# The last group's outputs in a buffer of their own, queries turned in pairs, one batch's loads held for another transfer, and a new order, in a fused linear-attention and gated-FFN kernel

## The chip, the cores and the metric

One core of one Trainium2 chip runs the whole program. The time is device microseconds of one execution. The kernel before took 301.0 us, the median of three runs (300.68 to 301.04).

## What is computed

Eight batches of eight heads, 576 positions, 64 values per head. Linear attention with cosine and sine weights, then a gated feed-forward layer over all 4608 tokens (512 wide, 1536 hidden):

```python
r = np.maximum(x, 0.0); phi = np.concatenate([r * c, r * s], axis=-1)   # for q and k
kv  = np.einsum('bhsf,bhsd->bhfd', k_p, v)
z   = np.sum(k_p, axis=2)
num = np.einsum('bhsf,bhfd->bhsd', q_p, kv)
den = np.einsum('bhsf,bhf->bhs', q_p, z)[..., None] + 1e-06
x   = (num / den).transpose(0, 2, 1, 3).reshape(B * S, H * D)
g   = x @ w_gate
out = (g * (1.0 / (1.0 + np.exp(-g))) * (x @ w_val)) @ w_out
```

Inputs and outputs are float32; the products run in 16-bit types with float32 sums.

## The kernel before, in words

**Tiles and groups.** Attention makes 36 token tiles of 128 tokens (two slots of 64; a batch has nine slots, so tile t holds slots 2t and 2t+1). Four tiles are a group of 512 tokens, and the feed-forward layer runs by group, 0 to 8. The gate, value and output products of the later groups are block products with seven instead of eight quarter products (a Strassen form): VectorE makes sums of the weights, of `xT` (L949) and of the hidden tiles (L1092), and TensorE accumulates into PSUM banks that ScalarE first fills with copies (L627).

**The path of a batch b from 2 on.** GpSimd issues the loads of k, v (L120) and q (L125), casting to bf16 on the way. ScalarE applies ReLU to k (L280), VectorE weighs v with the cosine/sine table (`vmul`, L292, four instructions a batch), TensorE makes the key-value products (`kv_job`, L715), ScalarE copies these into SBUF (L627, four copies). The features of q go into a buffer `r_q` (L866, L876, L282), and one DMA transpose from SyncE turns them into `phit` (L838). Then TensorE makes a tile (L784), ScalarE its denominator (L796), VectorE the reciprocal (L802) and the quotient `x` (L806, one of four slots), and SyncE's DMA transpose makes `xT` (L746). The products of a group read `xT` (L976 for block products, L1051 for whole ones).

**Tiles 4 to 8** belong to batches 0 and 1. Their queries are not turned by DMA: `turned_tile` has TensorE transpose 8 pieces of 128x64 for one tile into one bank (L1296), then ReLU (L280 or L282) and a weighting (L1310). In the program before, the turns of tiles 4 and 5 already stand next to each other; those of 6 and 7 stand apart.

**Held loads.** GpSimd's queue is in order. `hold_job` puts a 1x2 copy (L823) on it that reads something a transfer writes, so the loads behind it are issued only when that transfer has landed. The loads of batch 3 (k, v) and of batch 4 (q) are held for `phit` of batch 2.

**Outputs.** A group ends with seven output products (`out_jobs`, L1141). For the last group, products 6, 5 and 3 are split into two halves (P6, P5, P3 below), and VectorE and ScalarE bring the quarters into `ob` (L1184, L1198, L633, L629). `ob` has two places, each for a pair of tiles, used by every group in turn; a place is free when the stores of its last user have landed. Groups 1 to 7 store from GpSimd (L1110), the last group from SyncE and ScalarE (`store_two_jobs`, L1236). The quarter called `e11` in `out_jobs` comes from ScalarE, the two halves `e12` of the last product from VectorE.

**The order.** From the middle of group 0 on, the order of every engine's instructions is made when the program is built. Each piece of work is a `Job` with a duration for each engine that may run it, the jobs it follows, and the rooms (banks, slots, `ob` places) it takes and gives back. TensorE's jobs have keys that give a nominal order; due times are worked back from them, and a list scheduler (`order_once`) places all jobs, with a model of the DMA queue and with due times shifted at random by seeds. Only the order is kept: on the chip each engine runs its instructions in that order and waits on semaphores where data or room is missing.

Of the kernel before, what the change touches and what calls it, by code (L numbers as in the profile page):

```python
# [19 lines left out]
def kernel(  # L20
# [585 lines left out]
    def pe(occ, fn, key, **kw):  # L606
        return Job({"PE": occ}, fn, key=key, **kw)
# [135 lines left out]
    def turn_job(t, x, after, by_pe=False, key=None):  # L743
        if not by_pe:
            def fn(j):
                nc.sync.dma_start_transpose(out=xT_of(t), in_=one(x_all, x))  # L746
            J_["xT", t] = Job({"SP": 1450}, fn, after=after + J_.get(("xT_read", t // OUT - 3), []), put=[x], tail=X_LAND, dma=(1900.0, X_SVC))
            return
        r = Room("bank")

        def fn(j):
            ps = bank(r).bitcast(FP16).rearrange("p (k x) -> p k x", x=P)
            for kc in range(KC):
                nc.tensor.transpose(out=ps[:, kc], in_=one(x_all, x)[:, kc * P:(kc + 1) * P], identity=ident16)
# [61 lines left out]
    def load_job(b, nm, after, lands, behind):  # L816
        def fn(j):
            (load_turned if nm == "q" else load)(b, nm)
        J_["load", b, nm] = Job({"POOL": 1600 if nm == "q" else 780}, fn, after=after, tail=lands, behind=behind, dma=(2500.0, 3500.0))

    def hold_job(read, after):
        def fn(j):
            nc.gpsimd.tensor_copy(out=hold2, in_=read())  # L823
        jb = Job({"POOL": 480}, fn, after=after)
        jb.hold = True
        return jb

    def batch_jobs(b, key):
        def loaded(nm):
            return [J_["load", b, nm]] if b > 2 else []  # L830

        def landed_at(nm):
            return 0.0 if b > 2 else LOADED[nm, 2]
        phis = feature_jobs(b)

        def fn(j):
# [3 lines left out]
        turned = [Job({"SP": 7500}, fn, after=phis + J_.get(("tiles", b - 2), []), tail=PHI_LAND - 7500, dma=(2800.0, 6400.0))]  # L840
# [263 lines left out]
    def store_jobs(t, after, put, queues, cols=slice(0, d_model)):  # L1104
        for e in range(2):
            q_ = queues[e]

            def fn(j, e=e):
                idx = 2 * t + e
                {"POOL": nc.gpsimd, "SP": nc.sync, "ACT": nc.scalar}[j.eng].dma_start(  # L1110
                    out=out_v[idx // NC, idx % NC][:, cols], in_=ob_of(t)[e * SH:(e + 1) * SH, cols])
            Job({q_: 560}, fn, after=after, put=put, tail=6500.0, dma=(1900.0, 500.0))

    obs = {}

    def ob_of(t):
        return ob_all[:, obs[t // 2].at[0], t % 2]
# [113 lines left out]
    def store_two_jobs(t, cols, after, queues):  # L1231
        for e in range(2):
            def fn(j, e=e):
                (b, c), (b1, _) = divmod(2 * t + e, NC), divmod(2 * t + 2 + e, NC)
                assert b == b1
                {"SP": nc.sync, "ACT": nc.scalar}[j.eng].dma_start(  # L1236
                    out=out_v[b, c:c + 3:2, :, cols].rearrange("c p f -> p c f"),
                    in_=pair_of(t // 2)[e * SH:(e + 1) * SH, :, cols])
            Job({queues[e]: 560}, fn, after=after, tail=3000.0)

    def plain_out_jobs(key):
        rooms = [Room("ob"), Room("ob")]
# [39 lines left out]
    kv_job(1, (0, KV1_AT / 16), rk + vm)  # L1282
    plain_out_jobs((0, 0.76, 0.015))

    def turned_tile(t, key):

        r = Room("bank")
        slots = [(0, NC - 1), (1, 0)] if t == 4 else [(1, 2 * t - 9), (1, 2 * t - 8)]
        mine = late[:, 2 * (t % 2):2 * (t % 2) + 2]

        def fn(j):
            ps = bank(r).bitcast(BF16).rearrange("p (y e s) -> p y e s", e=2, s=SH)
            for jj in range(J):
                for n, (b, c) in enumerate(slots):
                    for i in range(2):
                        nc.tensor.transpose(out=ps[i * D:(i + 1) * D, 2 * jj + n].rearrange("p e s -> p (e s)"),  # L1296
                                            in_=raws[b, "q"][:, 2 * jj + i, c], identity=ident)
        mm = pe(240, fn, key, after=[], get=[r], rel=LOADED["sa" if t < 6 else "sb", 1])
        for b, c in slots:
            J_.setdefault(("q_read", b), []).append(mm)  # L1300
        old = J_["tile_mm"][-2:-1] if t > 5 else []

        def fn(j):
            relu_on(j.eng, mine[:, 0].rearrange("p e j c s -> p e (j c) s"),
                    bank(r).bitcast(BF16).rearrange("p (y e s) -> p e y s", e=2, s=SH)[:, :, 0:2 * J])
        re_ = Job({"ACT": sc(512), "DVE": 352}, fn, after=[mm] + old, put=[r])
        c0 = NC - 1 if t == 4 else 2 * t - 9

        def fn(j):
            tt(out=mine[:, 1].rearrange("p e j c s -> p (e j) (c s)"), in0=mine[:, 0].rearrange("p e j c s -> p (e j) (c s)"),  # L1310
               in1=tanT[:, c0:c0 + 2].rearrange("p c s -> p (c s)").unsqueeze(1).to_broadcast([P, 2 * J, P]), op=ALU.mult)
        J_["turned tile", t] = [re_, Job({"DVE": d2(512)}, fn, after=[re_])]

    J_["tile_mm"] = []
    for t in range(4, 9):
        turned_tile(t, (0, (HALF_AT[t - 4] - 0.6) / 16) if t < 8 else (0, T8_AT / 16))
        tile_jobs(t, (0, HALF_AT[t - 4] / 16) if t < 8 else (1, 1.0), t < 8)
        J_["tile_mm"].append(J_["tiles", 1][-1])
    J_["kvd_free"] = J_["tile_mm"][0:1]

    def fn_t(n):
# [53 lines left out]
    def batch_loads(read, after, names):  # L1375
        prev = [hold_job(read, after)]
# [58 lines left out]
    TILES_AT_ONCE = 2  # L1435
    DMA_MARGIN = 0.0
    EARLY = 9000.0
    SIZE = {"sg": NSG, "m7": NM7, "x": NX, "ob": 2, "tile": TILES_AT_ONCE}
    AHEAD = 18000.0
    SLACK = 1600.0  # L1440
    LOOSE = 8000.0
# [11 lines left out]
    def order_once(nominal, seeds):  # L1453
# [89 lines left out]
        while n_left:  # L1543
# [72 lines left out]
    SEEDS = (9809, 17028, 79282, 23851, 85677, 79440, 78841, 69575, 80126, 93490, 42418, 59393, 0, 20917, 95217, 13415, 85644, 62013, 51029, 24021, 0, 84984, 14392, 87705, 77482, 88068, 0, 0)  # L1616
    SHAKE = 1500.0
    WINDOW = 10000.0
    PACK = True
# [40 lines left out]
```

## Time and profile before

| what | value |
|---|---|
| time, median of three runs | 301.0 us (300.68 to 301.04) |
| the profiled execution's own time | 300.46 us |
| span in its profile | 298.7 us |
| granted TensorE clock | 0.998 |
| TensorE (PE) busy | 291.3 us, 98% |
| VectorE (DVE) busy | 250.9 us, 84% |
| ScalarE (ACT) busy | 199.5 us, 67% |
| GpSimd (POOL) busy | 70.6 us, 24% |
| first real product of TensorE / end of the last | 9.0 us / 293.4 us |
| key-value products of batch 3, start | 85.0 us |

The span runs from the first to the last instruction; 1.8 us of the execution's own time lie outside it. Matmuls are pipelined, so the distance from one start to the next tells more than a busy share: four products of 256 columns take 0.437 us from start to start when nothing holds them, four of 512 columns 0.863 us. Idle time in brackets stands before an instruction, with what ended it.

### The profile page before, as it was taken

What the parts mean: (1) busy time and instruction counts of PE and PEld (TensorE: products, weight loads), DVE (VectorE), ACT (ScalarE), POOL (GpSimd) and SP (SyncE); (2) the same over time, 40 slices, a digit from 0 to 9 for tenths busy, and PEclk for the clock granted to TensorE, in tenths of its full rate; (3) what the DMA queues carried; (4) which work ended last, traced back from release to release, by engine and by line L of the source; (5) the groups of instructions that cost most, each with busy time, mean ns of one, the idle gap of its engine ahead of it and who ended that gap; (6) DMA issues with size and microseconds to landing.
All of it is one profiled execution on the core that took longest, in us unless ns stands there. A gap on an engine that the chain in (4) does not pass through costs nothing.

```text
span 298.7 us, 8071 instructions
## 1 busy us (share of the span) xinstructions
PE 291.3 (98%) x3244; PEld 238.4 (80%) x3244; DVE 250.9 (84%) x513; ACT 199.5 (67%) x421; POOL 70.6 (24%) x126
## 2 busy tenths in 40 slices
PE   8999999999999999999999999999999999999992
PEld 4697465676777888888988888888888898888882
DVE  7878996978977898989979997988879868976972
ACT  6664346979558986797699588996475556645520
POOL 7954620030042130221233203200220050002020
PEclk9999999999999999999999999999999999999999
DMA  7999999999989999269899892770370074002025
GB/s 259 228 196 198 202 206 208 201 217 204 193 137 172 157 213 160 72 126 189 131 177 234 143 155 69 145 160 2 73 142 2 0 131 83 2 2 70 2 70 142
DMA packets 71781, 40.89 MB, mean 137 GB/s; under 512 B 48704, under 2 KB 68672, under 8 KB 71744
## 3 DMA queue, kind: packets, MB, share of 16 engines
q0 software_dynamic: 24992, 24.91, 49.8%
q1 hardware_dynamic: 46320, 15.08, 27.1%
q8 instruction: 25, 0.41, 0.6%
q10 hardware_dynamic: 432, 0.39, 0.4%
q14 instruction: 12, 0.10, 0.1%
HBM read 37.75 MB, written 9.44 MB: 158 GB/s over the span
## 4 chain that ended last, share of the span: by engine, by line
PE 88%; DVE 5%; DMA 4%; ACT 1%; issue 1%; ACTq 0%; DVEq 0%
PE banks L976 43%; PE banks L1141 23%; PE banks L1250 4%; PE banks L437 4%; PE banks L903 4%; DMA xT<-x 3%; PE banks L715 2%; PE banks L784 2%; PE banks L1051 2%; DMA wo_sb<-in_v_dram 1%; DVE ht L1060 1%; DVE sums L1092 1%; DVE v L292 1%; PE banks L778 1%; PE banks L371 1%; ACT sg L1035 1%
## 5 line engine op out<-in xcount | busy, mean ns | idle before, releaser
L1110 POOL DMA_DIRECT2D out_dram<-ob x56 | 29.4, 533 | 148.6 <-ACT ob L629 104.7
L1035 ACT ACTIVATE sg<-banks 128x512 bf16<-128x512 f32 x72 | 41.3, 596 | 9.9 <-PE banks L976 9.5
L627 ACT COPY banks<-banks 128x512 f32<-128x512 f32 (+1 forms) x53 | 30.2, 577 | 17.8 <-PE banks L1141 6.0
L1071 DVE TENSOR_TENSOR ht<-sg,banks 128x512 f16<-128x512 bf16 x60 | 40.3, 680 | 1.7 <-PE banks L976 1.6
L976 PEld LDWEIGHTS <-wg_sb 128*128 128x128 f16 x384 | 36.9, 98 | 5.5 <-issue 0.4
L1141 PEld LDWEIGHTS <-ht 128*128 128x128 f16 x384 | 37.0, 98 | 4.9 <-issue 0.3
L976 PEld LDWEIGHTS <-wgs_sb 128*128 128x128 f16 x368 | 35.6, 98 | 5.5
L996 DVE TENSOR_TENSOR banks<-m,banks 128x512 f32<-128x512 f32 x44 | 30.3, 691 | 7.0 <-ACT m L627 4.3
L629 ACT ACTIVATE ob<-banks 128x512 f32<-128x512 f32 x34 | 19.9, 595 | 22.7 <-PE banks L1141 22.3
L976 PEld LDWEIGHTS <-wv_sb 128*128 128x128 f16 x320 | 31.2, 98 | 3.9 <-DVE x L806 0.2
L976 PE MATMUL banks<-kvt,wgs_sb 128*128 128x256 f16 x236 | 33.6, 273 | 0.0
L1141 PEld LDWEIGHTS <-sums 128*128 128x128 f16 x288 | 27.9, 98 | 3.6 <-DVE sums L1092 0.2
L627 ACT COPY m<-banks 128x512 f32<-128x512 f32 x44 | 25.6, 589 | 6.5 <-PE banks L976 6.4
L976 PE MATMUL banks<-xT,wg_sb 128*128 128x256 f16 x192 | 28.5, 273 | 0.3 <-ACT banks L627 0.3
L1141 PE MATMUL banks<-wo_sb,ht 128*128 128x256 f16 x192 | 25.9, 273 | 0.0
L1141 PE MATMUL banks<-wt_sb,sums 128*128 128x256 f16 x192 | 24.3, 273 | 0.0
L976 PE MATMUL banks<-xT,wv_sb 128*128 128x256 f16 x160 | 23.9, 273 | 0.0
L806 DVE TENSOR_TENSOR x<-banks,rec 128x512 f16<-128x512 f32 x32 | 21.7, 687 | 2.0 <-DMA xT<-x 0.3
L976 PE MATMUL banks<-kvt,wg_sb 128*128 128x256 f16 x168 | 23.1, 273 | 0.0
L1141 PE MATMUL banks<-wt_sb,ht 128*128 128x256 f16 x192 | 22.8, 273 | 0.2 <-DVE banks L1184 0.2
L876 ACT ACTIVATE r_q<-raw_q,tanq 128x256 bf16<-128x256 bf16 x45 | 20.1, 503 | 0.0
L1035 ACT ACTIVATE sg<-m 128x512 bf16<-128x512 f32 x24 | 15.1, 629 | 7.1 <-DVE m L1004 7.0
(157 smaller groups left out, 542.4 us busy)
## 6 DMA issues: line engine op xcount, KB each, us to landing
out_dram<-ob POOLq DMA_DIRECT2D x56, 128.0 KB, 3.4
raw_kv<-in_k_dram POOLq DMA_DIRECT2D x7, 576.0 KB, 6.9
raw_q<-in_q_dram POOLq DMA_DIRECT2D x12, 288.0 KB, 9.6
raw_kv<-in_v_dram POOLq DMA_DIRECT2D x6, 576.0 KB, 8.9
out_dram<-ob SPq DMA_DIRECT2D x13, 128.0 KB, 2.5
wg_sb<-in_moe_w_gate_dram POOLq DMA_DIRECT2D x5, 256.0 KB, 8.8
wv_sb<-in_moe_w_val_dram POOLq DMA_DIRECT2D x5, 256.0 KB, 9.4
wo_sb<-in_v_dram SPq DMA_DIRECT2D x2, 576.0 KB, 4.1
```

What stands on the lines that cost most here:

```text
L437: nc.tensor.matmul(out=st["f", tg, fc, lo][i], lhsT=(wg_sb, wv_sb)[i][:, kc, fs], rhs=xT[tg][:, ts, kc], start=(kc == 0), stop=(kc == KC - 1))
L627: nc.scalar.copy(out=out, in_=in_)
L629: nc.scalar.mul(out=out, in_=in_, mul=mul)
L806: tt(out=one(x_all, x).rearrange("p (y e d) -> p e y d", e=2, d=D), in0=view()[:, :, :, 0:D], in1=rec_all[:, t % 4].rearrange("p (e y) o - ...
L876: nc.scalar.activation(out=home()[:, :, c, 1], in_=raws[b, "q"][:, :, c], func=AF.Relu, scale=tanq[:, c:c + 1])
L903: nc.tensor.matmul(out=bank(r), lhsT=w[:, kc, fc * P:(fc + 1) * P], rhs=xT[tg][:, :, kc], start=(kc == 0), stop=(kc == KC - 1))
L976: nc.tensor.matmul(out=to[:, i], lhsT=a[:, c, 2 * u + i], rhs=x()[:, :, c], start=first and i == 0 and c == 0, stop=c == KH - 1, skip_grou ...
L996: tt(out=bank(c), in0=one(m7_all, m).rearrange("p i x -> p (i x)"), in1=bank(b), op=ALU.add)
L1035: nc.scalar.activation(out=gates(rooms[w])[:, :, jh * HT:(jh + 1) * HT], in_=src, func=AF.Silu, scale=DOWN)
L1071: tt(out=ht[:, 4 * u + w:4 * u + w + 3:2, jh * HT:(jh + 1) * HT], in0=gates(rooms[w])[:, :, jh * HT:(jh + 1) * HT], in1=src.rearrange("p ( ...
L1110: {"POOL": nc.gpsimd, "SP": nc.sync, "ACT": nc.scalar}[j.eng].dma_start(out=out_v[idx // NC, idx % NC][:, cols], in_=ob_of(t)[e * SH:(e + ...
L1141: nc.tensor.matmul(out=to, lhsT=a[:, kc, i * P:(i + 1) * P], rhs=b[:, kc], start=first and kc == 0 and i == 0, stop=kc == HC - 1, skip_gro ...
```

## The change

- `rel`, the pool of `r_q`, is gone; `r_q` is a fixed buffer. The last group's outputs go into its first 8192 bytes per partition (`ob_last`, two places of the kind "last ob") and no longer into `ob`.
- `turned_tiles` turns the queries of tiles 4 and 5 in one job into one bank, and those of 6 and 7; tile 8 stays alone.
- The loads of batch 3 (k, v) and of batch 4 (q) are held for `xT` of tile 8, and no longer for `phit` of batch 2.
- The planner's figures for DMA change (durations, landing times, the delay `LATER`), its result counts the ends of all jobs, and the seeds are others. So the order of all engines from 27 us on is another.

TensorE has the same 3245 products and weight loads in both programs. In the new order the key-value products of batch 2 come about 2.5 us earlier, those of batch 3 about 4 us later, of batches 5 and 6 about 12.5 us earlier, of batch 7 about 7 us earlier. On SyncE's queue the turn of batch 5 stands between the transposes of tiles 16 and 19, 18, 17 (before: behind all four), and the transpose of tile 8 stands behind all six of group 0's stores that follow the turn of batch 2 (before: behind five). On GpSimd's queue the hold and the loads of k and v of batch 4 stand ahead of the stores of tiles 4 to 7 (before: between those of 6, 7 and of 4, 5), and k and v of batch 6 ahead of q of batch 6.

```diff
-    rel = ctx.enter_context(tc.tile_pool(name="rel", bufs=1))
+    rq_all = consts.tile([P, G * NC * 2 * D], BF16, name="r_q")
+    ob_last = rq_all[:, 0:8 * d_model].bitcast(FP32).rearrange("p (a b f) -> p a b f", a=2, b=2)
...
-            J_["xT", t] = Job({"SP": 1450}, fn, ..., tail=X_LAND, dma=(1900.0, X_SVC))
+            J_["xT", t] = Job({"SP": 1450}, fn, ..., tail=X_LAND, dma=(1430.0, X_SVC))
...
-    X_LAND = 7000.0
-    X_SVC = 1000.0
+    X_LAND = 4000.0
+    X_SVC = 1030.0
...
-        J_["load", b, nm] = Job(..., dma=(2500.0, 3500.0))
-    def hold_job(read, after):
+        J_["load", b, nm] = Job(..., dma=(1940.0, 2460.0) if nm == "q" else (470.0, 3770.0))
+    def hold_job(read, after, put=()):
...
-        turned = [Job({"SP": 7500}, fn, ..., tail=PHI_LAND - 7500, dma=(2800.0, 6400.0))]
+        turned = [Job({"SP": 7500}, fn, ..., tail=PHI_LAND - 7500, dma=(7600.0, 1370.0))]
...
-                st[b, "q"] = rel.tile([P, G, NC, 2, D], BF16, name="r_q")
+                st[b, "q"] = rq_all.rearrange("p (g c w d) -> p g c w d", g=G, c=NC, w=2)
...
     def pair_of(p):
-        return ob_all[:, obs[p].at[0]]
+        return (ob_last if obs[p].kind == "last ob" else ob_all)[:, obs[p].at[0]]
...
-        rooms = {0: Room("ob"), 1: Room("ob")}
+        rooms = {n: Room("last ob" if last else "ob") for n in range(2)}
...
-    def turned_tile(t, key):
+    def turned_tiles(ts, key):
         r = Room("bank")
...
+        def turned(m):
+            return bank(r).bitcast(BF16).rearrange("p (m y e s) -> p m y e s", m=2, e=2, s=SH)[:, m]
         def fn(j):
+            for m, t in enumerate(ts):
+                for jj in range(J):
+                    for n, (b, c) in enumerate(slots[t]):
+                        for i in range(2):
+                            nc.tensor.transpose(out=turned(m)[i * D:(i + 1) * D, 2 * jj + n].rearrange("p e s -> p (e s)"),
+                                                in_=raws[b, "q"][:, 2 * jj + i, c], identity=ident)
-        mm = pe(240, fn, key, after=[], get=[r], rel=LOADED["sa" if t < 6 else "sb", 1])
+        mm = pe(200 + 236 * len(ts), fn, key, after=[], get=[r], rel=LOADED["sa" if ts[-1] < 6 else "sb", 1])
...
-    for t in range(4, 9):
-        turned_tile(t, ...)
+    for ts in ((4, 5), (6, 7), (8,)):
+        turned_tiles(ts, ...)
...
-            batch_loads(phit_read, J_["turned", b - 1], names)
+            if b == 3:
+                batch_loads(lambda: xT[2][0:1, 0, 0, 0:2], [J_["xT", 8]], names)
+            else:
+                batch_loads(phit_read, J_["turned", b - 1], names)
...
-                j.done = moved[0] + LATER
+                j.done = moved[0] + (j.tail if j.tail < LATER else LATER)
-        return max(j.done for j in jobs if "PE" in j.engs)
+        return max(j.done for j in jobs)
-    LATER = 2200.0
-    SEEDS = (9809, 17028, 79282, 23851, ...)
+    LATER = 2400.0
+    SEEDS = (51094, 66641, 10020, 27923, ...)
```

More of the change, by code (lines that the diff above doesn't have):

```diff
@@ L746, in fn @@
                 nc.sync.dma_start_transpose(out=xT_of(t), in_=one(x_all, x))
-            J_["xT", t] = Job({"SP": 1450}, fn, after=after + J_.get(("xT_read", t // OUT - 3), []), put=[x], tail=X_LAND, dma=(1900.0, X_SVC))
+            J_["xT", t] = Job({"SP": 1450}, fn, after=after + J_.get(("xT_read", t // OUT - 3), []), put=[x], tail=X_LAND, dma=(1430.0, X_SVC))
             return
@@ L818, in fn @@
             (load_turned if nm == "q" else load)(b, nm)
-        J_["load", b, nm] = Job({"POOL": 1600 if nm == "q" else 780}, fn, after=after, tail=lands, behind=behind, dma=(2500.0, 3500.0))
-    def hold_job(read, after):
+        J_["load", b, nm] = Job({"POOL": 1600 if nm == "q" else 780}, fn, after=after, tail=lands, behind=behind, dma=(1940.0, 2460.0) if nm == "q" else (470.0, 3770.0))
+    def hold_job(read, after, put=()):
         def fn(j):
             nc.gpsimd.tensor_copy(out=hold2, in_=read())
-        jb = Job({"POOL": 480}, fn, after=after)
+        jb = Job({"POOL": 480}, fn, after=after, put=put)
         jb.hold = True
@@ L839, in fn @@
                                         in_=st[b, "q"].rearrange("p g c w d -> p (g c w d)"))
-        turned = [Job({"SP": 7500}, fn, after=phis + J_.get(("tiles", b - 2), []), tail=PHI_LAND - 7500, dma=(2800.0, 6400.0))]
+        turned = [Job({"SP": 7500}, fn, after=phis + J_.get(("tiles", b - 2), []), tail=PHI_LAND - 7500, dma=(7600.0, 1370.0))]
         J_["turned", b] = turned
@@ L1238, in fn @@
                     in_=pair_of(t // 2)[e * SH:(e + 1) * SH, :, cols])
-            Job({queues[e]: 560}, fn, after=after, tail=3000.0)
+            Job({queues[e]: 660}, fn, after=after, tail=1300.0, dma=(700.0, 560.0))
     def plain_out_jobs(key):
@@ L1283 @@
     plain_out_jobs((0, 0.76, 0.015))
-    def turned_tile(t, key):
+    def turned_tiles(ts, key):
         r = Room("bank")
-        slots = [(0, NC - 1), (1, 0)] if t == 4 else [(1, 2 * t - 9), (1, 2 * t - 8)]
-        mine = late[:, 2 * (t % 2):2 * (t % 2) + 2]
+        slots = {t: [(0, NC - 1), (1, 0)] if t == 4 else [(1, 2 * t - 9), (1, 2 * t - 8)] for t in ts}
+        def turned(m):
+            return bank(r).bitcast(BF16).rearrange("p (m y e s) -> p m y e s", m=2, e=2, s=SH)[:, m]
         def fn(j):
[L1292 to L1297, printed above, removed]
-        mm = pe(240, fn, key, after=[], get=[r], rel=LOADED["sa" if t < 6 else "sb", 1])
[L1299 to L1312, printed above, removed]
@@ new lines, in turned_tiles, with fn @@
+        mm = pe(200 + 236 * len(ts), fn, key, after=[], get=[r], rel=LOADED["sa" if ts[-1] < 6 else "sb", 1])
+        for t in ts:
+            for b, c in slots[t]:
+                J_.setdefault(("q_read", b), []).append(mm)
+        for m, t in enumerate(ts):
+            mine = late[:, 2 * (t % 2):2 * (t % 2) + 2]
+            old = J_["tile_mm"][t - 6:t - 5] if t > 5 else []
+            def fn(j, m=m, mine=mine):
+                relu_on(j.eng, mine[:, 0].rearrange("p e j c s -> p e (j c) s"), turned(m).rearrange("p y e s -> p e y s"))
+            re_ = Job({"ACT": sc(512), "DVE": 352}, fn, after=[mm] + old, put=[r])
+            c0 = NC - 1 if t == 4 else 2 * t - 9
+            def fn(j, mine=mine, c0=c0):
+                tt(out=mine[:, 1].rearrange("p e j c s -> p (e j) (c s)"), in0=mine[:, 0].rearrange("p e j c s -> p (e j) (c s)"),
+                   in1=tanT[:, c0:c0 + 2].rearrange("p c s -> p (c s)").unsqueeze(1).to_broadcast([P, 2 * J, P]), op=ALU.mult)
+            J_["turned tile", t] = [re_, Job({"DVE": d2(512)}, fn, after=[re_])]
@@ L1319 @@
+    J_["tile_mm"] = []
+    for ts in ((4, 5), (6, 7), (8,)):
+        turned_tiles(ts, (0, (HALF_AT[ts[0] - 4] - 0.6) / 16) if ts[0] < 8 else (0, T8_AT / 16))
+        for t in ts:
+            tile_jobs(t, (0, HALF_AT[t - 4] / 16) if t < 8 else (1, 1.0), t < 8)
+            J_["tile_mm"].append(J_["tiles", 1][-1])
     J_["kvd_free"] = J_["tile_mm"][0:1]
@@ L1373, in gate_order, with batch_loads @@
         return [at["g1"], at["g7"], at["g6"], at["g2"], at["g5"], at["g4"], nxt["g3p"]]
-    def batch_loads(read, after, names):
-        prev = [hold_job(read, after)]
+    def batch_loads(read, after, names, put=()):
+        prev = [hold_job(read, after, put)]
         for b, nm in names:
@@ L1437 @@
     EARLY = 9000.0
-    SIZE = {"sg": NSG, "m7": NM7, "x": NX, "ob": 2, "tile": TILES_AT_ONCE}
+    SIZE = {"sg": NSG, "m7": NM7, "x": NX, "ob": 2, "last ob": 2, "tile": TILES_AT_ONCE}
     AHEAD = 18000.0
```

9 lines of the change are left out of this document (3 added, 6 removed).

## The prediction

> **What bounds the kernel now.** I read the page's busy times and slices first, then TensorE's timeline, then the chain of waits and the timeline of the last 6 us. From the page, busy time (share of the span) and tenths in 40 slices:
>
> ```profile
> PE 291.3 (98%) x3244; PEld 238.4 (80%) x3244; DVE 250.9 (84%) x513; ACT 199.5 (67%) x421; POOL 70.6 (24%) x126
> ...
> PE   8999999999999999999999999999999999999992
> DVE  7878996978977898989979997988879868976972
> ```
>
> TensorE is the bound from the second slice to the last but one. Two things can move the time: TensorE's waits inside the stream, and the ends of the span. As a busy matmul row may hide a wait, I measured waits as the distance from one start to the next beyond the usual distance of the same work. From 26.9 us (the first instruction whose place the change may move) to 293.4 us, five waits exceed 0.16 us: 0.24 at 72.7, 0.34 at 81.7, 0.43 at 86.7, 0.20 at 127.9 and 0.19 us at 128.8, together 1.40 us. From 130 us on there is none beyond 0.1 us before the last products. The first three, in timelines of all engines and of PE (start, length, engine, line; in brackets the idle time and what ended it):
>
> ```profile
> 73.03 0.69 DVE L806 TENSOR_TENSOR x<-banks,rec 128x512 f16<-128x512 f32 x1 [0.26 <-DMA xT<-x]
> 73.77 0.11 PEld L1051 LDWEIGHTS <-wv_sb 128*128 128x128 f16 x2 [0.57 <-DVE x L806]
> ...
> 82.27 2.78 PE L1141 MATMUL banks<-wt_sb,ht 128*128 128x256 f16 x24 [0.17 <-DVE banks L1184]
> ...
> 87.52 0.60 PE L976 MATMUL banks<-xT,wg_sb 128*128 128x256 f16 x4 [0.27 <-ACT banks L627]
> ```
>
> The first is the transfer of tile 8: the chain of waits gives `xT<-x` 8.60 us from 64.31, while the transposes of `xT` land after 2.4/4.5/8.6 us (least, median, most). A quotient needed its slot, a bank came free late, TensorE waited, and VectorE, without a pause until 87 us, was late again at 82.
>
> The end (timeline, same columns):
>
> ```profile
> 293.40 0.42 DVE L633 TENSOR_SCALAR ob<-banks 128x256 f32<-128x256 f32 x1 [0.23 <-PE banks L1141]
> 293.74 0.60 ACT L629 ACTIVATE ob<-banks 128x512 f32<-128x512 f32 x1 [5.41 <-PE banks L1141]
> 293.86 1.28 SPq L1236 DMA_DIRECT2D out_dram<-ob  x2
> 293.90 1.66 ACTq L1236 DMA_DIRECT2D out_dram<-ob  x2
> ```
>
> Read it from the bottom: two queues issue two stores each, and the later store of each carries `e11` (the ScalarE row), which was placed behind the store of the quarter before it because its `ob` place had been the last to come free. The last product ends at 293.37 and its eviction at 293.83; the last store is issued at 294.93.
>
> **Part by part.** The sum is made against the profiled execution (span 298.7, own time 300.46 us), which lies 0.5 us under the median of the runs; differences are carried to that median.
>
> *Own buffer for the last group.* In the changed order ScalarE makes `e11` before it issues any store, and both its stores stand ahead of those of the third and last quarters. The last stores are then the two of `e12`, one on each queue, issued right behind VectorE's 0.42 us, as 293.86 and 293.90 are now. The last issue moves from 294.93 to 293.90: **-1.03 us**. Landing is the same (2.4/2.8/3.0 us for these stores). Ends: nothing, if the two stores' landing were late for another reason; -1.3, if they land at the 2.4 of a quiet queue and not at 2.8.
> The second half of product 2 moves ahead of product 6, so the first half of P5 stands directly behind P6. VectorE needs 0.27 us after P6's first half and 0.43 us (L1184: 288.45 to 288.88), the other half of P6 covers 0.65: **+0.1 us**. The cover is gone if VectorE is behind; it has 0.7 us to spare there, as its last hidden-tile sums follow fewer instructions.
>
> *Turning in pairs.* PE's timeline:
>
> ```profile
> 37.58 0.64 PE L1296 MATMUL banks<-ident,raw_q 128*64 128x128 bf16 x16
> ...
> 43.53 0.39 PE L754 MATMUL banks<-ident,x 128*128 128x128 f16 x4
> 43.85 0.41 PE L1296 MATMUL banks<-ident,raw_q 128*64 128x128 bf16 x8
> 44.20 0.40 PE L754 MATMUL banks<-ident,x 128*128 128x128 f16 x4
> 44.43 0.81 PE L1250 MATMUL banks<-wo_sb,ht 128*128 128x512 f16 x3
> ```
>
> Sixteen pieces in a row (tiles 4 and 5, already neighbours) take 0.56 us to the next start, eight alone 0.35; and the four L754 before a turn take 0.32 instead of the 0.23 of the next four. One pair newly joined: 2 x 0.35 - 0.56 + 0.09 = **-0.2 us**. Its bank is held longer and ReLU reads it twice, as before: two instructions each of ReLU and weighting in both programs, with 0.3 to 0.5 us to spare before tiles 6 and 7.
>
> *Loads of batch 3 held for tile 8.* The first two waits of before (0.58 us) should go. What is late next: the loads themselves. The turn of batch 2 ends its issue at 61.0, six stores of 0.62 follow, tile 8's transpose is issued at 64.9 and lands after the median 4.5 at 69.4; hold 0.18 and 0.36 until the first issue: k at 69.9 (before: 63.85), v at 70.7, q at 71.4 and 72.1. With before's own landing times (7.5, 10.2, 12.0 us) k is there at 77.4, v at 80.9, q at 84.1. GpSimd waits meanwhile; behind it stand only these loads. Before, v had landed 7.3 us ahead of its first use (82.12). Now the cover is thin: on VectorE one weighing of v (0.69) and two sums of `xT` (0.33 each) stand before group 2's second gate product, which PE's stream reaches at 84.1 if nothing waits. v may land at 82.6 at most, 1.7 us later than reckoned. Tiles 10 and 11 are issued at 69.8 and 71.1; even with 8.6 us they land by 79.7. Batch 3's key-value products come 4 us later, which costs nothing by itself.
>
> *Other moves on queues.* Batch 4's hold and loads ahead of four stores (0.53 each): their `ob` place is written again 20 us later. Batch 5's turn ahead of the transposes of tiles 19, 18, 17: it holds SyncE 4.5 to 7.6 us (L838), from about 125.5; tile 17 is issued at 132.6 to 135.7 and lands by 140.2 (4.5), at worst 142.1 (6.4, as after the first loads); its product stands at 141.6: 0 to 0.5 us, taken as 0. Key-value products of batches 5 and 6 move 12.5 us up; k and v of batch 5 landed at 120.4 before, 15 us ahead of the new place. `r_q` as a fixed buffer and the hold's other operand add no instruction.
>
> *The new order.* It places again all work from 27 us on, and what it waits for cannot be seen. Ends: no wait at all (-1.40; PE runs so from 130 to 292 us now), and three stretches like 72 to 87 us, which lost 1.0 us (3.0 us of waits, +1.6). I take the 1.40 us of before, its nearest row: the two waits that go are set against the thin cover of batch 3. **0.**
>
> Sum: -1.03 + 0.1 - 0.2 + 0 = -1.15 us: 299.3 for the profiled execution, and from the median **299.8 us**.
>
> **A rule that speaks against the hold.** Beside tile 8's 8.60 us, the next three transposes took 6.4, 6.1 and 5.4 us with the same loads still in flight. The Trainium skill, "DMA: Bandwidth & Descriptors", section Queues, rings and completion order, says that each DMA engine takes turns between the queues that have work for it, a packet at a time. By it the collision is only moved, to tiles 10 and 11, batch 3's own turn and the loads themselves; the trace agrees as far as it goes. That is the second rival.
>
> **The rivals.**
> *New waits eat it.* For it: ScalarE's and VectorE's work stands close ahead of its users everywhere (batch 3's copies 0.7 us ahead of tile 14, batch 5's 0.2 us ahead of tile 22). Against it: the same was true before, with 1.40 us lost. With 2.2 to 3.2 us of waits: 300.6 to 301.6.
> *Slower: batch 3's values arrive late.* They now share the DMA engines with tiles 10 and 11 and with the turn of batch 3 (issued at 72.4; 9.0 us median). For it: q of batch 3, beside a turn and behind other loads, took 18.1 us. Against: that load had three others ahead, this one has one. Each microsecond beyond 82.6 us is one of TensorE's. It ends slower than before by 0.6 once v lands beyond 84.4 (13.7 us after its issue, instead of 10.2); with 14.5 us the time is 302.4.
> *No waits left.* The new order runs as its stream adds up: 298.4. For it: 160 us of before do. Against: half of that part has no loads any more.
> *The end doesn't shorten.* Another store lands last: 300.9. Against: the four issue times above.
>
> **How the numbers follow.** Three runs of before spread over 0.36 us; 0.2% is 0.6 us, about what a measurement can tell from no change. Forecast (299.0 to 300.4) 0.48, no waits left 0.14: faster 0.62. New waits 0.18 and no shorter end 0.04: same 0.22. Late values: slower 0.16. The range 298.4 to 301.8 takes in the new order's ends and leaves out the outer part of the last rival.
>
> **What would show it.** Tail: ScalarE's last eviction ends before its first store, and last product to last issue falls from 1.6 to 0.5 us. Pairs: L1299's rows in three places (16, 16, 8). Hold: tile 8's transpose lands within 5 us, no VectorE wait on `xT` near 70, loads of batch 3 near 70. Wrong if VectorE waits for `raw_kv` before 84 us or ScalarE for q near 87, with TensorE idle behind, or if TensorE's waits beyond 0.16 us add up to over 2 us.

## The result, and the profile after

The changed kernel took 299.14 us (median of 10 executions, 298.34 to 301.42), the kernel before 301.05 us beside it (10 executions, 300.68 to 301.18): a ratio of 0.9946 with a 95% interval of 0.9923 to 0.9969. It is faster, by 0.3 to 0.8%. The forecast was 299.8 us, a ratio of 0.9960. The profiled execution took 299.61 us with a span of 297.8 us (before: 300.46 and 298.7).

The page of the changed kernel, with the rows of busy time and TensorE's tenths in 40 slices:

```profile
PE 291.9 (98%) x3244; PEld 239.1 (80%) x3244; DVE 252.7 (85%) x513; ACT 199.4 (67%) x421; POOL 71.5 (24%) x126
...
PE   8999999999999999999999999999999999999993
```

TensorE bounds the kernel as before, so the change is to be sought in TensorE's waits and at the ends of the span. I cut the spans (a second profile of the changed kernel comes from its repetition below) at the first instruction that the planner places and at the end of the last product:

| us | before | after | after, second profile |
|---|---|---|---|
| start to the first planned product | 26.91 | 27.75 | 27.41 |
| TensorE's stream from there to the last product's end | 266.46 | 265.47 | 265.24 |
| last product's end to the end of the span | 5.31 | 4.57 | 4.57 |
| span | 298.7 | 297.8 | 297.2 |

The first row is not the change's work: the instructions before 26.9 us are the same in both programs, and the row moves between executions of one kernel (last section). Without it the changed kernel's profiles are 1.7 and 2.0 us shorter, near the 1.9 us between the medians and more than the spans show.

**The end.** Timeline of the changed kernel's last 11 us (start, length, engine, line):

```profile
287.48 1.09 ACT L630 ACTIVATE r_q<-banks 128x512 f32<-128x512 f32 x2 [0.71 <-PE banks L1142]
...
292.66 1.64 SPq L1237 DMA_DIRECT2D out_dram<-r_q  x2
292.67 1.68 ACTq L1237 DMA_DIRECT2D out_dram<-r_q  x2
293.25 0.42 DVE L634 TENSOR_SCALAR r_q<-banks 128x256 f32<-128x256 f32 x1 [0.23 <-PE banks L1142]
```

ScalarE's last eviction ends at 288.57, ahead of its first store. The last product ends at 293.22, the last two stores are issued together at 293.71: 0.49 us, where it was 1.56.

**Pairs.** TensorE's timeline:

```profile
38.42 0.64 PE L1299 MATMUL banks<-ident,raw_q 128*64 128x128 bf16 x16
...
43.19 0.64 PE L1299 MATMUL banks<-ident,raw_q 128*64 128x128 bf16 x16
43.76 1.04 PE L1251 MATMUL banks<-wo_sb,ht 128*128 128x512 f16 x4
```

**Around the held loads.** Tile 8's transpose, issued at 64.90, landed after 3.7 us instead of 8.6, and VectorE's wait for it is gone. The loads were issued from 69.2 on. What became late are the transposes of tiles 10 and 11, issued at 70.9 and 72.3. First the chain of waits of the changed kernel from 70 to 90 us, then VectorE's and TensorE's timeline:

```profile
72.30 12.54 DMA xT<-x
...
84.96 0.77 DVE kvt L950 x2
...
85.78 1.05 PE banks L977 x8
```

```profile
84.96 0.76 DVE L950 TENSOR_TENSOR kvt<-xT 128x512 f16<-128x512 f16 x2 [1.79 <-DMA xT<-x]
...
85.78 1.05 PE L977 MATMUL banks<-kvt,wgs_sb 128*128 128x256 f16 x8 [0.15 <-DVE kvt L950]
```

Tile 10 landed after 9.7 us, tile 11 after 12.5 us, at 84.84. VectorE stood 1.79 us for it, and TensorE's start distance shows 0.32 us too many at this place. (`kvt` holds VectorE's sums of `xT`.) Distances more than 0.16 us beyond the usual are 0.32 here, 0.18 at 141 us and 0.28 at 242 us: 0.78 us in all, and 0.46 in the second profile (the last two alone), where before had 1.41.

### The profile page after: what moved, and what is told of

Read it like the earlier page. It is cut to its first block, busy times and chain, and to the rows that moved or that the text cites. A ratio compares the mean times of both kernels' runs of the same rounds, so it can differ in the third digit from the quotient of the medians.

```text
span 297.8 us, 8063 instructions
## 1 busy us (share of the span) xinstructions
PE 291.9 (98%) x3244; PEld 239.1 (80%) x3244; DVE 252.7 (85%) x513; ACT 199.4 (67%) x421; POOL 71.5 (24%) x126
## 4 chain that ended last, share of the span: by engine, by line
PE 90%; DMA 4%; DVE 2%; ACT 1%; issue 1%; DVEq 0%
PE banks L977 43%; PE banks L1142 22%; DMA xT<-x 4%; PE banks L1251 4%; PE banks L438 4%; PE banks L904 4%; PE banks L187 3%; PE banks L716 3%; PE banks L1052 2%; PE banks L785 2%; PE banks L779 1%; PE banks L372 1%; DVE x L807 1%; PE banks L1299 0%; PE banks L315 0%
## 5 line engine op out<-in xcount | busy, mean ns | idle before, releaser
L1111 POOL DMA_DIRECT2D out_dram<-ob x56 | 29.3, 531 | 119.4 <-ACT ob L630 84.1
L630 ACT ACTIVATE ob<-banks 128x512 f32<-128x512 f32 x32 | 18.8, 596 | 15.9 <-PE banks L1142 15.2
L1142 PE MATMUL banks<-wt_sb,sums 128*128 128x256 f16 x192 | 24.9, 273 | 0.0
L1036 ACT ACTIVATE sg<-m 128x512 bf16<-128x512 f32 x24 | 15.1, 630 | 12.5 <-DVE m L1005 12.4
L977 PE MATMUL banks<-kvt,wg_sb 128*128 128x256 f16 x168 | 22.4, 273 | 0.0
L877 ACT ACTIVATE r_q<-raw_q,tanq 128x256 bf16<-128x256 bf16 x45 | 20.7, 510 | 0.2 <-DMA phit<-r_q 0.2
## 6 DMA issues: line engine op xcount, KB each, us to landing
wo_sb<-in_moe_w_out_dram POOLq DMA_DIRECT2D x2, 512.0 KB, 12.5
```

The source lines that it names most:

```text
L630: nc.scalar.mul(out=out, in_=in_, mul=mul)
L877: nc.scalar.activation(out=home()[:, :, c, 1], in_=raws[b, "q"][:, :, c], func=AF.Relu, scale=tanq[:, c:c + 1])
L977: nc.tensor.matmul(out=to[:, i], lhsT=a[:, c, 2 * u + i], rhs=x()[:, :, c], start=first and i == 0 and c == 0, stop=c == KH - 1, skip_grou ...
L1036: nc.scalar.activation(out=gates(rooms[w])[:, :, jh * HT:(jh + 1) * HT], in_=src, func=AF.Silu, scale=DOWN)
L1142: nc.tensor.matmul(out=to, lhsT=a[:, kc, i * P:(i + 1) * P], rhs=b[:, kc], start=first and kc == 0 and i == 0, stop=kc == HC - 1, skip_gro ...
```

## The experiments

Theory A, after the result: the end gives some 0.75 us, the pair 0.2 us, and the new order, not the hold by itself, gives the rest by waiting less; the hold only moves a collision on the DMA engines from tile 8 to tiles 10 and 11. Rivals are named with each run. Every ratio is against the kernel before, run beside it.

### The changed kernel once more

> The changed kernel once more, to see what varies between its executions. Theory A: the spread of its times (298.3 to 301.4 us) comes from the transposes of tiles 10 and 11, which now share the DMA engines with batch 3's loads; their landing (80.6 and 84.8 us in the profile) moves from run to run, and VectorE's wait for xT before group 2's sums with it. Then this profile's own time differs from 299.6 by about as much as TensorE's wait at 84 us does. Rival B: the spread is that of the program's first 9 us (the changed kernel's first real product came 0.84 us later than before's), and the stream behind it is the same in every execution; then the wait at 84 stays at 0.3 us and the profiles differ by their start alone. Median expected 299.1 us by both.

298.48 us (298.28 to 299.00, 5 executions), ratio 0.9925 (0.9912 to 0.9938). Both theories have a part in it: the stream was 0.23 us shorter than in the first profile (tile 11 landed at 83.57, VectorE stood 0.87 us for it, TensorE nothing), and the start 0.34 us earlier. None of the five repeats the 300.6 and 301.4 us of the first ten.

### The hold undone, in the new order

```
-                batch_loads(lambda: xT[2][0:1, 0, 0, 0:2], [J_["xT", 8]], names)
+                batch_loads(phit_read, [J_["xT", 8]], names)
```

> The changed kernel in its own order, only the hold of batch 3's loads reads the turn of batch 2 again, as before. Theory A (the hold moves the collision from tile 8 to tiles 10 and 11, its gain is small): loads issued near 62 to 64 us; tile 8's transpose takes 8 to 9 us and a wait of 0.3 to 0.6 us comes near 70; tiles 10 and 11 land in 5 to 6 us instead of 9.7 and 12.5, VectorE's 1.8 us and TensorE's 0.3 us near 84 go. Time within 0.5 us of the changed kernel, with a smaller spread. Rival C (the hold is worth its price): tile 8 and then 9 late, 1 us or more slower than the changed kernel.

305.54 us (303.77 to 309.32, six executions; 305.10 without the longest), ratio 1.0154 (1.0123 to 1.0186): some 7 us slower than the changed kernel. Rival C is right, and far beyond its own number. The loads were issued at 63.4, tile 8 landed at 75.3 (9.4 us after its issue), tile 9 at 77.9. VectorE's and TensorE's timeline of this kernel:

```profile
75.40 0.69 DVE L807 TENSOR_TENSOR x<-banks,rec 128x512 f16<-128x512 f32 x1 [5.13 <-DMA xT<-x]
...
76.15 1.48 PE L1052 MATMUL banks<-xT,wv_sb 128*128 128x512 f16 x4 [3.75 <-DVE x L807]
```

A quotient needs the slot that tile 8's transpose reads, VectorE's queue stands behind it, TensorE behind VectorE. The waits do not end there: by stretches of this trace (PE, PEld, DVE, ACT, POOL, then the granted clock, DMA share, GB/s) TensorE came back at a lower clock:

```profile
72.00:76.00 4.00, 0.40 (x4) 0.20 (x3) 0.60 (x1) 0.11 (x1) 0.00 (x0) 1.00 1.21 197
76.00:78.00 2.00, 1.55 (x5) 0.55 (x5) 2.00 (x5) 0.68 (x2) 0.00 (x0) 0.64 1.32 170
78.00:80.00 2.00, 2.00 (x9) 1.24 (x9) 2.00 (x5) 1.57 (x4) 0.00 (x0) 0.50 0.80 59
```

Start distances that were 0.44 became 0.85 there. The stream is 5.75 us longer than in the changed kernel's second profile: 3.9 us of waiting for that quotient, 0.3 us for tile 9 behind it, and some 1.5 us of slow products.

### The hold alone, in the order before

```
-            batch_loads(phit_read, J_["turned", b - 1], names)
+            batch_loads((lambda: xT[2][0:1, 0, 0, 0:2]) if b == 3 else phit_read, J_["turned", b - 1], names)
```

> The kernel before in its own order, only the hold of batch 3's loads reads tile 8's transpose instead of the turn of batch 2; the counterpart of the changed kernel with its hold undone, which lost 7 us. Theory F (hold and order belong together: each order was laid out for its own hold, so crossing either loses): tile 8 lands in 2.4 to 4 us and the 0.24 us at 72.7 goes, but the loads come 4 to 5 us later, tiles 9 to 11 take 8 to 12 us, and new waits of 1 to 3 us come between 76 and 88: 301.5 to 303.5. Rival G (the hold is a gain by itself, as the prediction reckoned: 0.58 us of waits go): 300.2 to 300.4.

300.51 us (300.30 to 301.19, 11 executions), ratio 0.9991 (0.9982 to 1.0000). Rival G is nearer: tile 8 landed after 2.5 us and the wait at 72.7 is gone, while no new one came; tiles 9 to 11 took 7.4 to 5.8 us. But the second wait that the prediction counted with it is still there, in the same size (TensorE's timeline):

```profile
82.37 0.42 PE L784 MATMUL banks<-kv,phit 128*128 128x65 bf16 x8
82.96 2.78 PE L1141 MATMUL banks<-wt_sb,ht 128*128 128x256 f16 x24 [0.17 <-DVE banks L1184]
```

So the hold is worth about 0.25 us of stream in the order before, and some 7 us in the new one. The traces show why a late tile 8 costs so much more there. Counted from the first planned product, tile 8 lands 2.2 us later with the hold undone than in the kernel before, and VectorE is ready for the quotient that needs its slot 2.7 us earlier: VectorE waits 4.9 us more. The new order needs these loads held.

### Batch 4's queries apart from batch 3's keys and values

```
         def fn(j):
+            if (b, nm) == (4, "q"):
+                nc.gpsimd.tensor_copy(out=hold2, in_=xT[2][0:1, 3, 0, 0:2])
             (load_turned if nm == "q" else load)(b, nm)
```

> The changed kernel in its own order; the loads of batch 4's q stand behind a second hold, which waits for tile 11's transpose. Theory A (tiles 10 and 11 wait behind 1.2 MB of loads of k and v and 1.2 MB of q): without q beside them tiles 10 and 11 land 2 to 5 us earlier, VectorE's wait for xT near 84 falls from 1.8 us to under 0.5 us and TensorE's 0.3 us goes: 0.3 us faster than the changed kernel on the profile's own run, and a smaller spread. Rival D: the k and v loads alone fill the engines, tile 11 still lands near 84 us and nothing changes; then q, issued near 85, may be late for ScalarE (needed once the turn of batch 3 has landed, 89 us) and the time is 0 to 1 us longer.

298.93 us (298.45 to 299.35), ratio 0.9937 (0.9923 to 0.9951). The mechanism is as theory A has it: without the q loads beside them tiles 10 and 11 landed after 8.2 and 7.5 us, at 78.8 and 79.3, and VectorE's sums start without a wait:

```profile
82.04 0.75 DVE L293 TENSOR_TENSOR v<-raw_kv,tab 128x1152 bf16<-128x1152 bf16 x1
82.70 0.76 DVE L952 TENSOR_TENSOR kvt<-xT 128x512 f16<-128x512 f16 x2
```

But no time came of it: the wait that went had cost TensorE 0 to 0.3 us, and one of 0.40 us came at 154.6. Ahead of it stands VectorE's feature instruction for batch 6, which started at 153.75, once the second half of q had landed at 153.67. Whether that is this edit's doing is not shown: the run with tile 17 first has 0.40 us at the same product.

### All loads held for tile 11

```
         def fn(j):
+            if b == 3:
+                return
+            if (b, nm) == (4, "q"):
+                nc.gpsimd.tensor_copy(out=hold2, in_=xT[2][0:1, 3, 0, 0:2])
+                load(3, "k")
+                load(3, "v")
             (load_turned if nm == "q" else load)(b, nm)
```

> The changed kernel with the loads of batch 3 (k, v) and of batch 4 (q) held for tile 11's transpose instead of tile 8's, everything else in the same order. By the prediction's step, tiles 10 and 11 land in 2.4 to 4.5 us (near 74 and 76), v of batch 3 is issued near 77.5 and lands near 86, 3.5 us beyond the 82.6 us that TensorE's stream allows, and each microsecond beyond is one of TensorE's: 302 us. Rival N (VectorE's queue passes more than its own lateness on, as in the run with the hold on the turn, where tile 8 landed 6.7 us later and 6.3 us of waits followed): 303 to 306 us. Rival O (the values have more room than was reckoned): under 300 us.

306.24 us (two executions, 305.70 and 306.79), ratio 1.0171 (1.0151 to 1.0192). With no loads beside them tiles 8 to 11 landed after 2.42, 2.40, 2.41 and 2.49 us: this shows that the loads make the 9.7 and 12.5 us. Rival N has the size, but not the way. ScalarE's, VectorE's and TensorE's timeline:

```profile
84.99 1.25 ACT L281 ACTIVATE raw_kv<-raw_kv 128x576 bf16<-128x576 bf16 x2 [6.18 <-DMA raw_kv<-in_k_dram]
86.15 0.58 ACT L630 ACTIVATE ob<-banks 128x512 f32<-128x512 f32 x1
...
86.76 0.69 DVE L1191 SCALAR_TENSOR_TENSOR banks<-ob,banks 128x512 f32<-128x512 f32 x1 [6.80 <-ACT ob L630]
...
87.51 2.29 PE L1148 MATMUL banks<-wt_sb,ht 128*128 128x256 f16 x10 [5.43 <-DVE banks L1191]
```

It was k that held the chain, not v: ScalarE's ReLU of k (L281) stands ahead of an eviction (L630) in ScalarE's queue, VectorE needs the eviction, TensorE the bank. In the changed kernel this ReLU starts at 79.65 and k had landed at 75.6. v landed late as well, at 87.78, 5.2 us beyond the 82.6, so the size alone would fit late values too; but VectorE came to it only behind the eviction and stood 0.35 us for it. And again the clock was 0.50, from 86.5 to 93.3 us, which added 2.8 us to 5.6 of waiting.

### The own buffer undone, in the new order

```
-        rooms = {n: Room("last ob" if last else "ob") for n in range(2)}
+        rooms = {n: Room("ob") for n in range(2)}
```

> The changed kernel with the last group's outputs in the shared buffer again; TensorE's order is the same to the last product, ScalarE's last three evictions still stand ahead of its stores. Theory A: e11's eviction now waits until the stores of group 7 have landed in the place it takes (291.6 us in the profile of after), so that it and the stores behind it come later: 0.5 to 1.5 us slower than the changed kernel. Rival E: the place is free in time and the gain at the end came from the order alone: the same time within 0.2 us.

299.96 us (299.06 to 302.43, 12 executions), ratio 0.9980 (0.9959 to 1.0002): 1.5 us slower than the changed kernel beside it. The end is as theory A has it; ScalarE's timeline of the last 11 us:

```profile
289.45 0.60 ACT L630 ACTIVATE ob<-banks 128x512 f32<-128x512 f32 x1 [0.71 <-PE banks L1142]
293.34 0.60 ACT L630 ACTIVATE ob<-banks 128x512 f32<-128x512 f32 x1 [3.29 <-DMA out_dram<-ob]
294.64 2.56 ACTq L1237 DMA_DIRECT2D out_dram<-ob  x3
```

The eviction waits 3.29 us for the store of the place's last user. From the last product to the end it took 5.42 us (changed kernel: 4.57), so the buffer is worth 0.85 us of the 1.5; where a usual execution loses the other 0.6 us no trace shows. The profiled execution, 302.39 us, shows something else besides (TensorE's timeline):

```profile
141.83 1.47 PE L1142 MATMUL banks<-wt_sb,sums 128*128 128x256 f16 x12
145.70 0.50 PE L977 MATMUL banks<-xT,wg_sb 128*128 128x256 f16 x3 [2.40 <-DMA xT<-x]
```

TensorE waits for tile 17's transpose. Issued at 138.9, it landed at 145.66 instead of 143.3; the loads of batch 6 had been issued at 139.8, before it was out. In the changed kernel's two profiles it landed 0.05 and 0.5 us ahead of its use.

### The own buffer alone, in the order before

The buffer's lines of the change, and nothing else: `rq_all`, `ob_last`, `pair_of` and the rooms.

> The kernel before with the own buffer for the last group and nothing else: TensorE's, SyncE's and GpSimd's orders are the same, ScalarE makes e11 before its stores. Theory A (the buffer alone shortens the end): last product to last issue falls from 1.56 us to 0.5, the span by 0.75 to 1.0 us: 299.9 to 300.1 us, beside 300.86 for before. Rival E (the end was shortened by the order around it): no change, 300.9.

300.23 us (299.80 to 301.04, 11 executions), ratio 0.9974 (0.9964 to 0.9984), 0.78 us of 300.98. From the last product to the end it took 4.56 us, as in the changed kernel. TensorE's and VectorE's orders are those of before; only ScalarE, which no longer waits for a place, makes its last eviction ahead of its stores. Rival E falls: it is the buffer.

### The pair 6/7 split

```
             for m, t in enumerate(ts):
+                if t == 7:
+                    put_off.append(lambda m=m, t=t: one_tile(m, t))
+                else:
+                    one_tile(m, t)
...
+                while put_off:
+                    put_off.pop()()
```

(the second part stands behind an output product's matmuls.)

> The changed kernel with tile 7's eight transposes put behind the next two output products, so that the pair 6/7 is two runs of eight again; everything else in the same order. Theory A: 0.57 us becomes 0.35 + 0.35 plus an entry of 0.09: TensorE's stream 0.2 us longer, 298.7 us beside 298.48. Rival J: the 0.2 us is taken up by waits that follow (TensorE waits for data a little less): no change within 0.1 us of stream.

298.85 us (298.49 to 299.78), ratio 0.9936 (0.9922 to 0.9950). The two intervals overlap, so the time decides nothing; the trace does. TensorE's timeline:

```profile
42.32 0.41 PE L1302 MATMUL banks<-ident,raw_q 128*64 128x128 bf16 x8
42.67 0.60 PE L1253 MATMUL banks<-wo_sb,ht 128*128 128x512 f16 x2
43.20 0.41 PE L1302 MATMUL banks<-ident,raw_q 128*64 128x128 bf16 x8
43.55 0.60 PE L1253 MATMUL banks<-wo_sb,ht 128*128 128x512 f16 x2
```

From the tile before to the next tile's transposes the same work takes 2.83 us, in the changed kernel 2.61: 0.22 us, as reckoned. Whether all of it reaches the end is less clear: the whole stream took 265.37 us, 0.13 more than in the changed kernel's second profile and 0.10 less than in its first, so part of rival J may hold too.

### Two attempts to widen the thin margin at 142 us

Batch 6's loads held for tile 17 instead of the turn of batch 5:

```
-                batch_loads(phit_read, J_["turned", b - 1], names)
+                batch_loads((lambda: xT[4][0:1, 1, 0, 0:2]) if b == 6 else phit_read, J_["turned", b - 1], names)
```

> The changed kernel with one more hold moved the same way: batch 6's loads of k and v wait for the transpose of tile 17 instead of the turn of batch 5. In one execution (the shared buffer's run) they were issued at 139.8, while tile 17's transpose was still being issued; it took 6.8 us instead of 4.0 to 4.5, and TensorE waited 2.6 us at 142 for it. Theory H (the changed kernel's slow executions, 300.6 and 301.4 of 10, and two of 302.4 of the shared buffer's 12, are this collision): no execution above 299.2, median 298.3 to 298.5, loads issued near 143.5 with no wait for them behind. Rival I: batch 6's loads are now late for kv6 and the transposes of tiles 22 and 20, which take as long as before: 298.5 to 299.5 with waits near 155.

303.20 us (301.99 to 303.86), ratio 1.0076 (1.0057 to 1.0096): rival I, and worse. Tile 17 landed after 2.8 us, but k and v of batch 6 were issued 1.6 us later and q 1.2 us, counted from the first planned product (27.00 here, 27.75 in the changed kernel's first profile). The second half of q landed at 155.74, 2.8 us later on that count; in the changed kernel it lands at 153.72 and VectorE's feature instruction starts on it at 153.81, so there was no room at all. VectorE's queue stands behind it, and TensorE's timeline shows

```profile
157.53 1.03 PE L977 MATMUL banks<-kvt,wv_sb 128*128 128x256 f16 x8 [2.14 <-DVE banks L997]
```

and then, from 158.5 on, products at half their rate; the granted clock is 0.50 from 158.5 to 161.9 us.

The transposes of tiles 17, 19, 18 in this order (`put_off` collects tiles 18 and 19 and issues them behind tile 17):

> The changed kernel with SyncE's transposes of tiles 17, 19, 18 in this order instead of 19, 18, 17 behind the turn of batch 5; nothing else moves. Theory H (the slow executions come from tile 17, which lands 143.1 to 143.3 us in two profiles and is needed by TensorE at 143.3 to 143.8, and 145.7 in a slow one): tile 17 lands near 140.5, no execution waits for it; the last of the three now only feeds VectorE's sums (first used at 145.2), so that a slow execution loses 1 us instead of 2.6: median 298.3 to 298.6, none above 300. Rival L: VectorE's sum of tiles 18 and 19 stands first in its queue and now waits 0.7 us more in every execution, with what is behind it: 298.7 to 299.5.

298.64 us (298.52 to 299.72), ratio 0.9926 (0.9912 to 0.9939): the same as the changed kernel. Rival L shows in VectorE's and TensorE's timeline:

```profile
143.15 0.76 DVE L956 TENSOR_TENSOR kvt<-xT 128x512 f16<-128x512 f16 x2 [0.58 <-DMA xT<-x]
...
144.30 0.61 PE L1148 MATMUL banks<-wt_sb,sums 128*128 128x256 f16 x4 [0.18 <-DVE sums L1099]
```

The delay that is taken from TensorE's product falls on VectorE's sum. Whether the rare long executions are tile 17's stays open: of the changed kernel itself none was profiled.

### The same three parts in two other orders

With the planner's figures, delay and seeds of before:

> The changed kernel's three parts (own buffer, pairs, hold for tile 8) with the figures, the delay and the seeds of the planner before, so with another order. Theory K (the order is worth as much as the parts: the new figures and seeds were what let it run with 0.3 us of waits): TensorE's waits beyond 0.16 us add up to 2 to 6 us and the time is 300.5 to 304. Rival M (the parts carry the gain, any order of the planner is about as good): 298.3 to 299.3.

315.34 us (311.50 to 315.42), ratio 1.0442 (1.0399 to 1.0485).

With the new figures and `SEEDS = (0,)`:

> The changed kernel with its own figures, but no seeds: due times are not shifted at random. Theory K: waits of 2 to 8 us, 301 to 307 us. Rival M: 298.3 to 299.3.

316.32 us (315.39 to 319.70), ratio 1.0493 (1.0477 to 1.0509). What TensorE waited for in the first and in the second of them (engine, line, what; us in total, times, longest):

```profile
PE banks L977 <- DVE sums L1093: 2.8, 1, 2.8
PE banks L785 <- ACT ob L630: 2.2, 1, 2.2
```

```profile
PE banks L977 <- DVE kvt L950: 5.5, 1, 5.5
PE banks L977 <- DMA xT<-x: 3.5, 1, 3.5
```

Theory K holds, well beyond its own numbers: start distances beyond 0.16 us add up to 13.0 us in 16 places, and 18.2 us in 30 (among them products at half rate behind a long wait), against 0.8. Rival M falls: the parts do not carry the gain in every order of the planner. These two are not two fair samples of orders, though: one list of seeds belongs to the program before, whose own order runs in 301 us, and the other is no list at all. And the new figures and seeds without the three parts were not run, so the new order's own share is what is left when the others are taken off, and not a measured difference.

## Why the prediction was right, and where it was wrong

The direction, the chance that led and the range were right; the time was forecast 0.7 us too long, and about 1.2 us against the second measurement. That second one, 298.48 us, lies outside the leading forecast's 299.0 to 300.4 and at the 298.4 of the rival "no waits left", though waits of 0.46 us were left. Luck has a part in the forecast: the buffer's term was too large and the new order's too small, and the two errors partly cancel. (Two small slips of the sum: its -1.15 counts the pair at the unrounded -0.23, and landing at 2.4 instead of 2.8 us would have made -1.4 of the buffer's term and not -1.3.)

- **Own buffer, -1.03.** The mechanism is as told, the size 0.2 to 0.3 us too large. The last issue did move by 1.07 us against the last product. "Landing is the same" failed: the last store to land took 2.98 us instead of 2.83 (the nearest row of before, ScalarE's store at 293.90, had taken 3.00), and from its landing to the end of the span it took 1.10 us instead of 0.91, for which no run shows a reason. Measured: -0.78 alone, -0.85 undone. The +0.1 behind P6 came out as reckoned: P6's second half takes 0.755 us to P5's start, 0.655 before.
- **Pair, -0.2.** Right on the spot: 0.22.
- **Hold.** The step that gave it two waits (0.58 us) was wrong by one: the wait at 81.7 was not the consequence of tile 8, since it stays at 0.33 when tile 8 is on time. The arrival of the loads was reckoned well (k 77.4, v 80.9, q 84.1; measured 75.6, 80.0 and 83.3 to 84.6). The bound "even with 8.6 us they land by 79.7" for tiles 10 and 11 failed: 8.60 was the landing of a transpose with one of these loads issued ahead of it, while three stood ahead of tile 10 and four ahead of tile 11, and these took 9.7 and 12.5 us. That cost VectorE 0.9 to 1.8 us and TensorE only 0 to 0.3. The second rival, late values, named the place; in the run that brought it about (all loads held for tile 11) it was ScalarE's ReLU of k that gave way first.
- **The rule that speaks against the hold.** The prediction drew from it that the collision would only be moved, and so it was: tiles 10 and 11 landed after 2.4 to 2.5 us with no loads in flight, and after 9.7 and 12.5 us with three and four issued ahead of them. The Trainium skill, "DMA: Bandwidth & Descriptors", section Queues, rings and completion order, says that each DMA engine takes turns between the queues; these landings fit that, but no run shows the turns themselves.
- **Other queue moves, 0.** Right in the usual execution, with less room than reckoned: tile 17 landed at 143.1 to 143.3, not by 142.1. The turn of batch 5 was issued at 127.1 to 127.7 and not at 125.5, and the two transposes ahead of tile 17 took 3.7 to 4.1 us to issue and not 2.6. The 2.4 us of idle time seen once shows the price.
- **New order, 0.** This is the term that failed most: waits of 1.41 us became 0.78 and 0.46, so it is worth -0.6 to -0.95, the hold's 0.25 included (the first rival's opposite, half-way or more to "no waits left"). With the end, the pair and the +0.1 that makes 1.5 of the first profile's 1.7 us and 1.8 of the second's 2.0; the last 0.2 us lie in distances too small for the list and were not followed. Its ends, -1.4 and +1.6, were no bounds either: two other orders of the same parts wait 13 and 18 us. The profile of before could not tell which of these orders was at hand; that the forecast came out is owed to an order that waits little, not to the argument that before's waits are the nearest row.

## What to carry to other kernels

A hold, an order and a buffer of a densely planned program are not parts with prices of their own: the same hold was worth 0.25 us in one order and 7 us in the other. Price a moved load by the first instruction of any in-order queue that reads it (here the ReLU of k ahead of an eviction), not by the engine that uses it in the end. Where a place in a buffer comes free only when a store has landed, that store belongs to the last group's critical path; giving that group a place of its own gained 0.8 us here, in both orders.

## What the runs showed of the hardware

- A wait of TensorE can cost more than itself. After 3.75 and 5.43 us of idle time (hold undone, all loads held for tile 11) the granted clock was 0.50 for 3.4 and 6.8 us. Waits of 2.84 and 2.16 us (the planner's old figures) and of 2.14 us (batch 6's loads held) led to 0.50 as well, but 2.40 us (shared buffer) did not. The clock records of all fourteen traces explain this: after the first release the granted clock changes only at whole multiples of 3.413 us from it. Of the windows at full clock inside TensorE's stream, the seven with 2.09 to 3.41 us of idle time were each followed by a clock of 0.50, and none with 1.64 us or less was. The 2.14 us lay in one window; the 2.40 us were cut by a window's end into 0.78 and 1.64. (Idle times are the profile's, whose ends of products are modelled.) The Trainium skill, "TensorE: Matmul & The Clock Gate", section Part 1: The HAM clock gate, says that an idle window of about 3.4 us halves the clock; the length of the window agrees, but here 2.09 us of idle time in it were enough.
- The same code up to the first planned product took 26.82 to 27.91 us in fourteen profiles of programs whose first 26 us are alike. TensorE starts with products of zeros; the first twelve of them run at 0.43 us each until the full clock is granted. Between 6 and all 12 did so, and the clock came at 3.7 us in one profile and past 6.4 us in three; in these three the first planned product came latest (27.75 to 27.91 us), while among the other eleven its place, 26.82 to 27.41, hardly follows the clock. The same section of the Trainium skill says that the window runs freely and does not start with the kernel, so that the point of release differs between executions by half a microsecond to each side, and tells of 6, 11 or 14 slow products in one kernel; here the point lies between 3.7 and 6.8 us, with 6 to 12 slow products. So up to 1.1 us between two spans is no effect of a change; it has to be taken off before two profiles are compared.
